# Retention and a gated feed-forward layer on one core: the order of three small products, and seven block products in place of eight for the second chunk

## The chip, the cores and the metric

The kernel runs on one core of a Trainium2 chip. A core has TensorE (matrix products, into PSUM), VectorE, ScalarE, GpSimd, and queues for the DMA engines. The metric is the device time of one execution in microseconds (us), smaller is better. In the listings of the profile PE is TensorE, PEld its loading of weights, DVE VectorE, ACT ScalarE, POOL GpSimd, SP the queue that issues most transfers.

## The reference

Eight batches, eight heads, 576 tokens, head size 64, all in float32. First comes a retention layer (attention with a decay in place of softmax), then a feed-forward layer with its own activation:

```python
# q, k, v: (8, 8, 576, 64); w_in: (512, 2048); w_out: (2048, 512)
scores = (1 / np.sqrt(64)) * np.matmul(q, k.transpose(0, 1, 3, 2))
gamma = 1.0 - 2.0 ** (-5.0 - np.arange(H))
Dmat = np.where(rel >= 0, gamma[:, None, None] ** rel[None], 0.0)   # rel = i - j
attn = np.matmul(scores * Dmat[None], v)
x = attn.transpose(0, 2, 1, 3).reshape(4608, 512)
h = x @ w_in
sp = np.maximum(h, 0.0) + np.log1p(np.exp(-np.abs(h)))             # softplus
g = h * erf(sp)
out = g @ w_out
```

The weights w_in and w_out arrive in double precision, and the kernel itself rounds them to float32 ("rounding" below).

## The kernel before

**Retention by pieces.** The 4608 tokens are cut into 36 pieces of 128. Within a piece the kernel computes masked scores; what earlier pieces of the same batch contribute comes through a state (64 by 64 for each head). Each piece i has three stages: `transposes(i)` brings q and k into the layout that the products need, `scores(i)` multiplies them and VectorE applies the mask, `outputs(i)` computes the piece's outputs and the new state:

```python
def outputs(i):
    ...
    o = [ps_at.tile([P, NP, P], FP32, tag="at", name=f"o{j}") for j in range(2)]
    for p in range(NP):                      # line 365: outputs within the piece
        for e in range(2):
            nc.tensor.matmul(o[p % 2][heads[(e + p) % 2], p // 2, :],
                lhsT=t["v"][:, 2 * p + e, :], rhs=t["sT"][:, e, p, :], ...)
    for state, r0, m in seen:                # line 376: what the state adds
        for p in range(NP):
            for e in range(2):
                nc.tensor.matmul(o[p % 2][heads[(e + p) % 2], p // 2, r0 : r0 + m],
                    lhsT=state[heads[e], p, :], rhs=t["qT"][heads[e], p, r0 : r0 + m], ...)
    if n == P:                               # line 388: the new state's product, k times v
        kv = flat(o[0])[:, 2 * P :].rearrange("p (a d) -> p a d", a=NP)
        for p in range(NP):
            for e in range(2):
                nc.tensor.matmul(kv[heads[e], p, :],
                    lhsT=t["k"][:, 2 * p + e, :], rhs=t["v"][:, 2 * p + e, :], ...)
    ...
    scaled(1)                                # VectorE: half of the outputs into x
    if n == P:
        sums = kv
        if s0 > 0:
            tt(sums, kv, kept[b], ALU.add)   # VectorE
        (nc.gpsimd if s0 > 0 else nc.vector).tensor_tensor(out=new, in0=sums, in1=gp, op=ALU.mult)
        kept[b] = new
    scaled(0)                                # VectorE: the other half
```

`seen` is empty in the first piece of a batch; the last piece of two batches at a time is shared by them (two states, no new state).

**The big products.** The tokens go through in nine chunks of 512, and the hidden columns in four groups (g = 0 to 3). For each group and chunk, `First` computes h, the activation is applied, and `Second` multiplies by w_out and adds to the output. Each is a product of 2 by 2 blocks. It is done by seven block products instead of eight, with sums of blocks made beforehand (Winograd's form of Strassen's method); VectorE makes the sums of x (`operands_x`), of the weights (`sums_in`, `sums_out`) and of g (`sums`). One block product is four `matmul` calls of 256 columns, which the profile records as eight. The first two chunks of the first group use the plain form instead, 16 steps of two calls:

```python
def plain(self):                             # line 550
    ...
    for dc in range(n_dc):
        slots = (A12, A22) if dc // 2 else (A11, S3)
        for n in range(4):
            for j in range(GP):
                nc.tensor.matmul(acc[n][:, ...], lhsT=wa[:, slots[n % 2], dc % 2, ...], rhs=t[:, dc, ...], ...)
            if dc == n_dc - 1:
                nc.scalar.copy(out=(self.t2 if tok else self.t1)[:, f], in_=acc[n])
            yield

def first(self):                             # the seven products, line 496
    self.product(A11, self.a, True);  nc.scalar.copy(out=self.t1[:, 0], in_=self.a)
    yield
    self.product(A12, e, True);       tt(self.t1[:, 0], e, self.t1[:, 0], ALU.add)
    yield
def middle(self):
    self.product(S2, self.a, False);  nc.scalar.copy(out=self.t1[:, 1], in_=self.a)
    yield
    self.product(S3, self.e, True)
    yield
    self.product(S1, self.a, False);  nc.scalar.copy(out=self.t2[:, 1], in_=self.a)
    tt(self.t2[:, 1], self.e, self.t2[:, 1], ALU.add)
    yield
def last(self):
    self.product(S4, self.a, False);  nc.scalar.copy(out=self.t2[:, 0], in_=self.a)
    yield
    self.product(A22, self.e, False); tt(self.t1[:, 1], self.e, self.t1[:, 1], ALU.add)
    self.softplus()
    yield

def operands_x(g, c):
    ...
    if g == 0 or c < PLAIN:                  # PLAIN = 2: chunks stored without the sums
        tt(t1, b12, b11, ALU.subtract)
        tt(t2, b22, t1, ALU.subtract)
        tt(b12, b22, b12, ALU.subtract)
    else:
        tt(t2, b12, b11, ALU.add)
        tt(t1, b22, t2, ALU.subtract)
    if g == 0:
        store_x(c)
    tt(t4, b21, t2, ALU.subtract)
```

**Rounding.** Each group has four parts of w_in and four of w_out. One part takes five steps: (1) two ScalarE instructions, (2) to (4) one VectorE instruction each, (5) a VectorE instruction and two on GpSimd (on VectorE for the first group's w_in). After the last part of w_out come four VectorE instructions for its sums; in the first group the four for w_in's sums come only behind those.

**The order of it all.** Engines work through their instructions in program order, so the program interleaves the work by hand. A string of letters steers the start (`a` one stage of attention, `p` one plain step of the first chunk, a digit so many rounding steps, `w` loading weights, `s` storing x). Then comes the second chunk:

```python
attend(after_chunk(1))                       # all stages that the second chunk needs
store_x(1)
for step, _ in enumerate(firsts[1].plain()):
    if step % 2 == 0:
        attend(min(done[0] + 1, most[0]))    # one stage of attention
    round_weights(int(step > 1))
    if step == 1:
        firsts[0].softplus(); firsts[0].erf()    # ScalarE, first chunk
    elif step == 5:
        firsts[0].multiply()                     # VectorE
    elif step == 8:
        firsts[0].sums()                         # VectorE
seconds[0].begin()
run(seconds[0].first(), (2, 2))              # a stage and two rounding steps with each product
firsts[1].softplus()
```

Of the kernel before, what the change touches and what calls it, by code (L numbers as in the profile page):

```python
# [2 lines left out]

# [1 line left out]

# [16 lines left out]
NP = H // 2  # L22
# [32 lines left out]
def kernel(  # L55
# [10 lines left out]
    nc = tc.nc  # L66
# [5 lines left out]
    n_dc = D_MODEL // P  # L72
    OH = D_MODEL // 2
    FH = D_FF // 2
    GP = 2
# [22 lines left out]
    def tt(out, in0, in1, op):  # L98
        nc.vector.tensor_tensor(out=out, in0=in0, in1=in1, op=op)  # L99

    def flat(ap):
        return ap.rearrange("p h d -> p (h d)")

    heads = [slice(e * D, (e + 1) * D) for e in range(2)]
# [87 lines left out]
    def parts():  # L192

        w2 = w_in.rearrange("(e c d) (h f) -> c e d h f", c=n_dc, d=D, h=2)
        for g in range(n_g):
            for dc in range(n_dc):
                a = A11 if dc < 2 else A12
                src = [(heads[(e + dc) % 2], w2[dc, e, :, :, 2 * g * GW : 2 * (g + 1) * GW]) for e in range(2)]

                yield src, "wa", g, a, dc % 2, ["wa"] if g > 0 and dc == n_dc - 1 else []  # L200
            for f in range(2):
                for j in range(GP):
                    ft = f * FH // P + g * GP + j
                    src = [(slice(0, P), w_out[ft * P : (ft + 1) * P, :].rearrange("p (h o) -> p h o", h=2))]
                    sums = (["wb"] if g > 0 else ["wb", "wa"]) if (f, j) == (1, GP - 1) else []
                    yield src, "wb", g, B21 if f else B11, j, sums

    def sums_in(a11, s3, a12, a22, s1, s2, s4):
# [79 lines left out]
    def round_weights(n=1):  # L288
        for _ in range(n):
            next(round_step, None)  # L290
# [9 lines left out]
    def x_tile():  # L300
        return xpool.tile([P, n_dc + 3, TCH], FP32, tag="x", name="x")
# [52 lines left out]
    def outputs(i):  # L354
        segments = pieces[i]
        t = live.pop(i)
        seen = [(kept[b], r0, n) for b, s0, n, r0 in segments if s0 > 0]

        b, s0, n, _ = segments[0]
# [3 lines that stand above are left out]
                nc.tensor.matmul(  # L365
                    o[p % 2][heads[(e + p) % 2], p // 2, :],
                    lhsT=t["v"][:, 2 * p + e, :],
                    rhs=t["sT"][:, e, p, :],
                    start=(p < 2),
                    stop=(not seen and p >= NP - 2),  # L370
                    skip_group_check=True,
                )
        for state, r0, m in seen:
            for p in range(NP):
                for e in range(2):
                    nc.tensor.matmul(  # L376
                        o[p % 2][heads[(e + p) % 2], p // 2, r0 : r0 + m],
                        lhsT=state[heads[e], p, :],
                        rhs=t["qT"][heads[e], p, r0 : r0 + m],
                        start=False,  # L380
                        stop=(p >= NP - 2),
                        skip_group_check=True,
                    )
        if n == P:
            kv = flat(o[0])[:, 2 * P :].rearrange("p (a d) -> p a d", a=NP)
            for p in range(NP):
                for e in range(2):
                    nc.tensor.matmul(  # L388
                        kv[heads[e], p, :],
                        lhsT=t["k"][:, 2 * p + e, :],  # L390
                        rhs=t["v"][:, 2 * p + e, :],
                        start=False,
                        stop=(p == NP - 1),
                        skip_group_check=True,
                    )
        c, at = i // PC, i % PC * P
        if (0, c) not in x:
            x[0, c] = x_tile()

        def scaled(j):  # L400
            to = x[0, c][:, j:NP:2, at : at + P]
            if c < n_ch - 1:
                by = (gq if n == P else gq2)[:, j::2, :].unsqueeze(2).to_broadcast([P, 2, P // n, n])
                dst, got = (y.rearrange("p a (m i) -> p a m i", i=n) for y in (to, o[j][:, :2]))
                tt(dst, got, by, ALU.mult)
                return

            for r0 in range(0, P, n):
                dst = to[:, :, r0 : r0 + n].rearrange("p h (r a) -> p h a r", r=SQ)
                got, by = (  # L410
                    y.rearrange("p h (a r) -> p h a r", r=SQ)
                    for y in (o[j][:, :2, r0 : r0 + n], (gq if n == P else gq2)[:, j::2, :])
                )
                tt(dst, got, by, ALU.mult)

        scaled(1)
        if n == P:
            sums = kv
            if s0 > 0:
                sums = att.tile([P, NP, D], FP32, tag="sums", name="sums")  # L420
                tt(sums, kv, kept[b], ALU.add)

            if b % 2 == 0 and s0 + P + D == S:
                new = att.tile([P, NP, D], FP32, tag="last", name="last", bufs=1)
            else:
                new = att.tile([P, NP, D], FP32, tag="state", name="state")
            (nc.gpsimd if s0 > 0 else nc.vector).tensor_tensor(out=new, in0=sums, in1=gp, op=ALU.mult)
            kept[b] = new
        scaled(0)
        load(i + 3, "kv")  # L430
        if i + 1 >= SQUARES:
            weigh_values(i + 1)
# [7 lines left out]
    done = [0]  # L440
# [5 lines left out]
    def after_chunk(c):  # L446

        return stages.index((outputs, (c + 1) * PC - 1)) + 1

    def attend(upto):  # L450
        while done[0] < min(upto, len(stages)):
            of, i = stages[done[0]]
            of(i)
            done[0] += 1

    PLAIN = 2

    def load_x(g, c):  # L460
        x[g, c] = x_tile()
# [2 lines left out]
    def store_x(c):  # L464
        nc.sync.dma_start(out=xd[c], in_=x[0, c][:, :n_dc])
# [3 lines left out]
    def operands_x(g, c):  # L469
        summed.add((g, c))  # L470
        t = x[g, c]
        b11, b12, b21, b22 = (t[:, 2 * d : 2 * d + 2, h * TH : (h + 1) * TH] for d in range(2) for h in range(2))
        t1, t2, t4 = (t[:, n_dc + j, :].rearrange("p (d i) -> p d i", d=2) for j in range(3))
        if g == 0 or c < PLAIN:
# [9 lines that stand above are left out]
        x[g, c] = {A11: b11, A12: b21, S4: b22, A22: t4, S1: t1, S2: t2, S3: b12}  # L484
# [240 lines left out]
    firsts = [First(g, c) for g, c in order]  # L725
    seconds = [Second(f) for f in firsts]
# [8 lines left out]
    def keep_busy(n):  # L735
        for _ in range(n):
            nc.tensor.matmul(idle[:, :P], lhsT=ones, rhs=ones, start=True, stop=True)
# [4 lines left out]
    def run(steps, rounds=(), stages=1):  # L742

        for step, _ in enumerate(steps):
            attend(min(done[0] + stages, most[0]))
            round_weights(rounds[step] if step < len(rounds) else 0)
# [4 lines left out]

    for what in "alkakakawkakakawwaa3awa2aaa5ppppaa5wwppa5ppawappwcppa5ppaaapp5s":
        if what == "a":
            attend(done[0] + 1)
        elif what == "p":
            next(products)
        elif what == "s":
            store_x(0)  # L760
        elif what == "l":
            load(2, "kv")
        elif what == "c":
            nc.sync.dma_start(out=cst[:, CONST_FIRST:], in_=consts[:, CONST_FIRST:])
        elif what == "w":
            load_weights()
        elif what == "k":
            keep_busy(2)
        else:
            round_weights(int(what))  # L770
    most[0] = before_chunk(3)
    attend(after_chunk(1))
    store_x(1)
    for step, _ in enumerate(firsts[1].plain()):
        if step % 2 == 0:
            attend(min(done[0] + 1, most[0]))
        round_weights(int(step > 1))
        if step == 1:
            firsts[0].softplus()
            firsts[0].erf()  # L780
        elif step == 5:
            firsts[0].multiply()
        elif step == 8:
            firsts[0].sums()
    seconds[0].begin()
    run(seconds[0].first(), (2, 2))
    firsts[1].softplus()
    most[0] = before_chunk(4)
    for b, nxt in zip(blocks[2:], blocks[3:] + [None]):
        n = order.index((b.g, b.c))  # L790
# [9 lines left out]
        elif n + 2 < n_s:  # L800
            f = firsts[n + 1]
# [62 lines left out]
```

## Time and profile before

| | before |
|---|---|
| median of three runs | 1027.61 us (1027.31 to 1028.06) |
| span of the profiled execution | 1024.0 us |
| TensorE matmul records, busy | 6348, 1017.6 us |
| VectorE instructions, busy | 1062, 667.6 us |
| ScalarE instructions, busy | 481, 390.2 us |
| GpSimd instructions, busy | 122, 122.6 us |

The busy time of an engine is the sum of what its instructions took. For TensorE, the end of a matmul is modelled, and a matmul that waits in the middle of a group makes the group look longer; the distance from one group's start to the next is the better measure. In a list in order of time, each line has the start, the time, the engine, the source line, the operation, what is written and read, the shape, and the number of instructions merged into it; a bracket at the end names an idle time before it and what ended it. In a list of waits, each line has who waited for whom, the total in us, how often, and the longest. A "wait for issue" is idle time for which the profile shows no partner.

### The profile page before, as it was taken

How to read it: one execution, taken by the hardware profiler on the slowest of the kernel's cores; microseconds unless marked ns; L12 is line 12 of the kernel's file. 1: busy time of each engine (PE TensorE's matmuls, PEld its weight loads, DVE VectorE, ACT ScalarE, POOL GpSimd, SP SyncE). 2: the span in 40 equal slices, each digit the busy share in tenths (PEclk: the TensorE clock that was granted, in tenths of full speed). 3: DMA queues.
4: the chain of work that ended last, by engine and by line, in shares of the span. 5: the costliest groups of instructions: out<-in, count | busy, mean ns of one | idle time of the engine just before them, and what ended most of it. 6: DMA issues, size and time to landing. Idle time of an engine off the chain costs nothing.

```text
span 1024.0 us, 15958 instructions
## 1 busy us (share of the span) xinstructions
PE 1017.6 (99%) x6348; PEld 876.0 (86%) x6348; DVE 667.6 (65%) x1062; ACT 390.2 (38%) x481; POOL 122.6 (12%) x122
## 2 busy tenths in 40 slices
PE   9999999999999999999999999999999999999998
PEld 8787888888888888888888888888888888888887
DVE  3769777976976656656666666666567655555555
ACT  3354134234134444334343444444433333333332
POOL 2143112122312110010001001000100000000000
PEclk9999999999999999999999999999999999999999
DMA  9998989979974354544444345444433333444434
GB/s 200 203 242 175 232 203 223 255 150 253 244 195 150 106 161 145 165 160 154 164 147 158 124 147 162 165 144 144 144 124 124 124 131 127 131 136 131 126 88 119
DMA packets 146986, 165.76 MB, mean 162 GB/s; under 512 B 97376, under 2 KB 121568, under 8 KB 138848
## 3 DMA queue, kind: packets, MB, share of 16 engines
q1 hardware_dynamic: 144832, 163.57, 56.4%
q10 hardware_dynamic: 2080, 1.18, 0.5%
q8 instruction: 50, 0.82, 0.4%
q14 instruction: 24, 0.20, 0.1%
HBM read 117.52 MB, written 47.19 MB: 161 GB/s over the span
## 4 chain that ended last, share of the span: by engine, by line
PE 94%; DMA 3%; DVE 2%; SPq 1%; POOL 1%; issue 0%; ACTq 0%; DVEq 0%; POOLq 0%
PE a L604 24%; PE a L496 23%; PE g L604 12%; PE g L496 12%; PE e L496 6%; PE e L604 6%; PE o L365 3%; PE s L347 3%; PE o L388 2%; DMA raw_k<-in_k_dram 1%; PE o L376 1%; DMA raw_v<-in_v_dram 1%; PE f L668 1%; SPq L147 1%; PE p L550 1%; PE h L668 1%
## 5 line engine op out<-in xcount | busy, mean ns | idle before, releaser
L496 PE MATMUL a<-x,wa 128*128 128x256 f32 x1088 | 258.3, 380 | 0.0
L496 PEld LDWEIGHTS a<-x,wa 128*128 128x128 f32 x1088 | 205.7, 190 | 28.5
L604 PE MATMUL a<-wb,s 128*128 128x256 f32 x840 | 200.0, 381 | 0.0
L604 PEld LDWEIGHTS a<-wb,s 128*128 128x128 f32 x840 | 158.4, 190 | 22.9 <-ACT o L618 0.7
L99 DVE TENSOR_TENSOR t<-g,t 128x512 f32<-128x512 f32 x68 | 47.0, 691 | 151.9 <-ACT t L526 114.1
L496 PE MATMUL g<-x,wa 128*128 128x256 f32 x544 | 129.2, 380 | 0.0
L496 PEld LDWEIGHTS g<-x,wa 128*128 128x128 f32 x544 | 102.8, 190 | 14.4
L99 DVE TENSOR_TENSOR o<-a,o 128x512 f32<-128x512 f32 x104 | 71.4, 687 | 46.4 <-PE a L604 46.4
L521 ACT COPY t<-a 128x512 f32<-128x512 f32 x34 | 19.9, 586 | 188.3 <-PE a L496 188.3
L99 DVE TENSOR_TENSOR t<-t,s 128x1024 f32<-128x1024 f32 x72 | 88.4, 1267 | 0.0
L274 POOL TENSOR_TENSOR wraw<-wraw 128x512 f32<-128x512 f32 x28 | 29.4, 1051 | 438.1 <-DVE wraw L272 184.4
L565 ACT ACTIVATE s<-t 128x1024 f32<-128x1024 f32 x72 | 72.1, 1049 | 24.6 <-DVE t L99 24.5
L99 DVE TENSOR_TENSOR x<-x 128x512 f32<-128x512 f32 x115 | 75.8, 693 | 1.2
L532 ACT COPY t<-a 128x512 f32<-128x512 f32 x34 | 19.9, 586 | 144.4 <-PE a L496 144.4
L569 ACT ACTIVATE s<-s 128x1024 f32<-128x1024 f32 x72 | 72.1, 1049 | 0.4
L604 PE MATMUL g<-wb,s 128*128 128x256 f32 x280 | 66.7, 381 | 0.0
L604 PE MATMUL e<-wb,t 128*128 128x256 f32 x280 | 66.6, 380 | 0.0
L604 PE MATMUL a<-wb,t 128*128 128x256 f32 x280 | 66.6, 380 | 0.0
L604 PE MATMUL g<-wb,t 128*128 128x256 f32 x280 | 66.4, 380 | 0.0
L99 DVE TENSOR_TENSOR sT<-s,cst 128x512 f32<-128x512 f32 x72 | 46.2, 682 | 30.4 <-PE s L347 30.4
L496 PE MATMUL e<-x,wa 128*128 128x256 f32 x272 | 64.8, 381 | 0.0
L99 DVE TENSOR_TENSOR o<-g,o 128x512 f32<-128x512 f32 x70 | 47.9, 684 | 20.9 <-ACT o L618 18.1
(86 smaller groups left out, 1247.1 us busy)
## 6 DMA issues: line engine op xcount, KB each, us to landing
od<-o SPq DMA_DIRECT2D x54, 512.0 KB, 3.3
x<-xd SPq DMA_DIRECT2D x27, 1024.0 KB, 4.8
o<-od SPq DMA_DIRECT2D x27, 1024.0 KB, 5.4
raw_qs<-in_q_dram SPq DMA_DIRECT2D x96, 112.0 KB, 4.4
raw_ks<-in_k_dram SPq DMA_DIRECT2D x84, 112.0 KB, 4.2
xd<-x SPq DMA_DIRECT2D x9, 1024.0 KB, 5.2
raw_v<-in_v_dram SPq DMA_DIRECT2D x64, 128.0 KB, 4.5
wraw<-in_moe_w_in_dram SPq DMA_DIRECT2D x32, 256.0 KB, 5.7
```

Source lines behind the costliest of these rows:

```text
L99: nc.vector.tensor_tensor(out=out, in0=in0, in1=in1, op=op)
L274: engine.tensor_tensor(out=r_f, in0=high_f, in1=r_f, op=ALU.mult)
L347: nc.tensor.matmul(ps[e][:, p, :], lhsT=t["kT"][heads[e], p, :], rhs=t["qT"][heads[e], p, :], start=True, stop=True)
L365: nc.tensor.matmul(o[p % 2][heads[(e + p) % 2], p // 2, :], lhsT=t["v"][:, 2 * p + e, :], rhs=t["sT"][:, e, p, :], start=(p < 2), stop=(no ...
L388: nc.tensor.matmul(kv[heads[e], p, :], lhsT=t["k"][:, 2 * p + e, :], rhs=t["v"][:, 2 * p + e, :], start=False, stop=(p == NP - 1), skip_gr ...
L496: nc.tensor.matmul(acc[:, j * TH : (j + 1) * TH], lhsT=weights["wa", self.g][:, a, d, j * P : (j + 1) * P], rhs=x[self.g, self.c][a][:, d, :],
L521: nc.scalar.copy(out=self.t1[:, 1], in_=self.a)
L532: nc.scalar.copy(out=self.t2[:, 0], in_=self.a)
L565: nc.scalar.activation(self.s[:, j], t, AF.Softplus)
L569: nc.scalar.activation(self.s[:, j], self.s[:, j], AF.Erf)
L604: nc.tensor.matmul(acc[:, tp, :], lhsT=left[:, j * TH + tp * P : j * TH + (tp + 1) * P], rhs=weights["wb", self.g][:, b, j, :], start=(sta ...
L668: nc.tensor.matmul(acc, lhsT=left[:, j * TH + tp * P : j * TH + (tp + 1) * P], rhs=weights["wb", self.g][:, b, j, :], start=(b in (B11, B2 ...
```

## The change

Two things are done. In `outputs`, the product for the new state moves directly behind the products for the outputs, and VectorE makes the sum for the new state ahead of both halves of the outputs; it is meant to give the next piece its state sooner. The second chunk now goes through the seven products like all later ones; for this the sums of w_in follow directly on its rounding, four more rounding steps stand in the steering string, one stage of attention is done ahead of the chunk, and the rounding steps are spread as 0, 2, 2, 2, 4, 2, 2 over the seven products, so that w_out is complete, with its sums, when `seconds[0]` begins. As x of the second chunk is now stored with its sums, the later groups make one sum fewer for it (`PLAIN = 1`).

```diff
-                yield src, "wa", g, a, dc % 2, ["wa"] if g > 0 and dc == n_dc - 1 else []
+                yield src, "wa", g, a, dc % 2, ["wa"] if dc == n_dc - 1 else []
...
-                    sums = (["wb"] if g > 0 else ["wb", "wa"]) if (f, j) == (1, GP - 1) else []
+                    sums = ["wb"] if (f, j) == (1, GP - 1) else []
...                                          (in outputs)
-        for state, r0, m in seen:
-            ...                              (line 376, moved)
         if n == P:
             kv = flat(o[0])[:, 2 * P :].rearrange("p (a d) -> p a d", a=NP)
             ...                              (line 388)
+        for state, r0, m in seen:
+            ...                              (line 376)
...
-        scaled(1)
         if n == P:
             sums = kv
             ...
             kept[b] = new
+        scaled(1)
         scaled(0)
...
-    PLAIN = 2
+    PLAIN = 1
...
-    for what in "alkakakawkakakawwaa3awa2aaa5ppppaa5wwppa5ppawappwcppa5ppaaapp5s":
+    for what in "alkakakawkakakawwaa3awa2aaa5ppppaa5wwppa5ppawappwcpp4a5ppaaapp5s":
...
     attend(after_chunk(1))
-    store_x(1)
-    for step, _ in enumerate(firsts[1].plain()):
-        if step % 2 == 0:
+    attend(done[0] + 1)
+    operands_x(0, 1)
+    f = firsts[1]
+    for step, _ in enumerate(chain(f.first(), f.middle(), f.last())):
+        if step > 0:
             attend(min(done[0] + 1, most[0]))
-        round_weights(int(step > 1))
-        if step == 1:
+        round_weights((0, 2, 2, 2, 4, 2, 2)[step])
+        if step == 0:
             firsts[0].softplus()
             firsts[0].erf()
-        elif step == 5:
+        elif step == 2:
             firsts[0].multiply()
-        elif step == 8:
+        elif step == 4:
             firsts[0].sums()
     seconds[0].begin()
-    run(seconds[0].first(), (2, 2))
-    firsts[1].softplus()
+    run(seconds[0].first())
```

More of the change, by code (lines that the diff above doesn't have):

```diff
@@ L2 @@
 from contextlib import ExitStack
+from itertools import chain
 import numpy as np
@@ L372, in outputs @@
                 )
-        for state, r0, m in seen:
[L374 to L383, printed above, removed]
         if n == P:
@@ L393, in outputs @@
                         stop=(p == NP - 1),
+                        skip_group_check=True,
+                    )
+        for state, r0, m in seen:
+            for p in range(NP):
+                for e in range(2):
+                    nc.tensor.matmul(
+                        o[p % 2][heads[(e + p) % 2], p // 2, r0 : r0 + m],
+                        lhsT=state[heads[e], p, :],
+                        rhs=t["qT"][heads[e], p, r0 : r0 + m],
+                        start=False,
+                        stop=(p >= NP - 2),
                         skip_group_check=True,
```

## The prediction

> **What bounds the kernel now.** I read the page first, then TensorE's waits, then its list of instructions in order of time, and last the lists of VectorE and ScalarE beside it. From the page, the busy shares and the chain that ended last:
>
> ```profile
> PE 1017.6 (99%) x6348; PEld 876.0 (86%) x6348; DVE 667.6 (65%) x1062; ACT 390.2 (38%) x481; POOL 122.6 (12%) x122
> ...
> PE 94%; DMA 3%; DVE 2%; SPq 1%; POOL 1%; issue 0%; ACTq 0%; DVEq 0%; POOLq 0%
> ```
>
> TensorE never stops for long, and the chain is TensorE. But a busy TensorE is not one at its peak: a matmul that waits inside a group shows as a longer group. So I used the distance between starts. TensorE in order of time (start, modelled length, line; line 347 is the scores, 365 the outputs, 376 the product with the state, 388 the new state's product, 496 and 604 the big products):
>
> ```profile
> 84.59 0.60 PE L332 MATMUL pt_k<-ident,raw_k 128*128 128x128 f32 x4
> 85.03 1.89 PE L604 MATMUL e<-wb,t 128*128 128x256 f32 x8
> 86.85 1.61 PE L365 MATMUL o<-sT,raw_v 128*64 128x128 f32 x16
> 88.39 0.67 PE L376 MATMUL o<-qT,state 64*64 64x128 f32 x16
> ...
> 114.08 1.09 PE L365 MATMUL o<-sT,raw_v 128*64 128x128 f32 x16
> 115.00 0.63 PE L388 MATMUL o<-raw_v,raw_k 128*64 128x64 f32 x16
> 115.56 1.99 PE L496 MATMUL a<-x,wa 128*128 128x256 f32 x8
> ...
> 165.41 1.09 PE L365 MATMUL o<-sT,raw_v 128*64 128x128 f32 x16
> 166.44 0.67 PE L376 MATMUL o<-qT,state 64*64 64x128 f32 x16
> 167.03 0.69 PE L388 MATMUL o<-raw_v,raw_k 128*64 128x64 f32 x16
> 167.65 1.99 PE L496 MATMUL g<-x,wa 128*128 128x256 f32 x8
> ```
>
> The outputs at 86.85 took 1.54 us to the next start (88.39) where undisturbed ones take 1.03: a stall of 0.51, and VectorE's mask just then ran from 86.04 to about 87.3. The rest is even. From 98.5 to 311.9 us, where attention lies between products, every kind of step repeats to 0.01 us; after 314 us a product of eight records follows the other at 1.73 us with two exceptions of 0.10, until the last at 1018.49. So nothing off TensorE matters after 98 us, and the end moves by what TensorE's work and its stalls before 98 us change, plus a small amount for each later piece of attention.
>
> **The skill.** Trainium skill, "TensorE: Matmul & The Clock Gate", section The mechanism: a weight load overlaps running matmuls of another row group, each tile of the array holding its own weights. The trace shows gaps where the tile shape changes; TensorE's weight loads waited:
>
> ```profile
> PEld o L365 <- issue: 10.4, 33, 0.5
> PEld s L347 <- issue: 9.0, 27, 0.3
> PEld o L376 <- issue: 4.8, 28, 0.2
> PEld o L388 <- issue: 3.6, 21, 0.2
> ```
>
> The fourth line is what I need. Line 388 runs in 32 pieces; 24 follow line 376, eight follow line 365 at once, and the 21 waits are about as many as the first kind. Both 365 and 388 are 128*64, 376 is 64*64. Second, "SBUF — State Buffer", section Who interferes with whom: a VectorE instruction with two SBUF inputs blocks against a GpSimd one that reads SBUF. The trace agrees: one such 128x512 instruction at 76.00 took 1.77 us and not 0.69, with GpSimd's add at 75.81 lasting 1.41. Third, "ScalarE: Activation LUTs", section What ACT_TABLE_LOAD costs: about 1283 ns; the trace has 1.28.
>
> **Part 1: seven products for the second chunk.** Before: 16 steps of four records, 64 records. After: seven products of eight, 56. Eight records by 1.73/8 = 0.216 us take **1.73 us** off TensorE, all of it on the path. One stage of attention now stands next to another and not between products; each entry or exit of such a run costs a product 0.10 (1.73 alone, 1.83 with one, 1.92 with both), so I take another 0.15.
>
> **Part 2: order inside the outputs.** Before, a piece with a state costs 1.03 (365 to 376) + 0.60 (376 to 388) + 0.615 (388 to a product) = 2.24 us. After, 365 to 388 is 0.92, as at 114.08. Then 388 to 376: 388 alone is 0.565, as at 115.00, plus the 0.10 that 365 pays when 376 follows = 0.665. Then 376 to a product: I take 0.55 to 0.60, since it now is 0.60 toward 388, and half-width ones part from a product with 0.34 against 0.28 between themselves. Sum 2.14 to 2.19, a gain of 0.05 to 0.10 each; VectorE's instruction "sums" has count 24, so 24 such pieces: 1.2 to 2.4, middle **1.8 us**. The stated purpose, an earlier state, brings nothing: no line of TensorE's waits names the state.
>
> **Part 3: VectorE and ScalarE from 60 to 98 us.** In that stretch VectorE is busy 31.05 of 38.00 us. Added: four combinations of x (4 x 0.69 = 2.8, start to start nearer 2.4) and three additions from PSUM (3 x 0.69 = 2.1). Removed: the sums of w_in, which filled 89.07 to 90.4 and 91.95 to 94.3, about 3.8 us with blocking; they move to the gap of 3.45 us ahead of 49.54 and cost nothing there. VectorE so carries some 32 us in a stretch that TensorE wants to make 2 us shorter. The trouble is its order:
>
> ```profile
> 64.22 1.29 DVE L99 TENSOR_TENSOR sT<-s,cst 128x512 f32<-128x512 f32 x2 [1.69 <-PE s L347]
> 69.21 0.43 DVE L259 TENSOR_SCALAR wb<-wb 128x512 f32<-128x512 f32 x1 [3.69 <-ACT wb L254]
> ...
> 79.02 0.68 DVE L99 TENSOR_TENSOR s<-t,s 128x512 f32<-128x512 f32 x1
> 79.62 0.42 DVE L263 TENSOR_SCALAR wb<-wb 128x512 uint32<-128x512 uint32 x1
> 79.96 0.70 DVE L326 STREAM_TRANSPOSE qT<-raw_qs 128x512 f32<-128x512 f32 x1
> ```
>
> The rounding at 69.21 waits until ScalarE has done softplus and erf with two table loads (1.28 + 2.00 + 1.28 + 2.00, from 61.98 to 68.5). That stays about the same, since ScalarE still starts near 62. From there I laid the new order end to end with these lengths: rounding and transpose to 71.7; multiplication 2.3 to 74.0; outputs, rounding, addition and mask to 76.8; four rounding steps 1.85 to 78.7; four sums of the first chunk 2.4 plus 1.1 blocked by GpSimd to 82.2; transpose of tenth q to **82.9**. TensorE reaches the scores of that piece, now behind the first product of the second stage, at about **81.4**: stall 1.5 us. Before that, the fifth product needs the accumulator that ScalarE copies behind the rounding's two instructions (69.0 to 70.2, copy to 70.8), while TensorE is there at 70.35: stall 0.6. Other small ones 0.3. Set against these, the present stalls of 0.27 (scores at 80.81) and 0.51 (outputs at 86.85) go or are counted in: net **+1.6 us**, the most uncertain term.
>
> **Sum.** -1.73 - 0.15 - 1.8 + 1.6 = -2.1 us; 1027.6 - 2.1 = 1025.5.
>
> **Later.** One VectorE addition fewer for the second chunk in each of three later groups (three instead of four) is off the path: no stalls there.
>
> **Rivals.** (a) VectorE becomes the bound of the stretch: a lag of 4 us at the tenth transpose eats both gains, and the time is 1027.5 to 1028.5. For it: VectorE's 31 of 38 us, its strict order, waits for GpSimd. Against: about 3.7 of the idle time stands in one place ahead of 69.21, and x's combinations fit in there; the removed sums of w_in free 3.8 us at 89 to 94, where a lag is made good. (b) The stalls don't come and both gains stay: 1023.5 to 1024. For it: before, VectorE was equally full from 70 to 80 us (4.96 and 4.97 of 5.00) and TensorE stalled 0.27. Against: the tenth transpose now has four rounding steps, two additions and the combinations ahead of it. (c) The order inside the outputs brings nothing, as the two shape changes only move (376 to a product costs what 388 to a product did plus one change): 1027.3. Against: the eight direct cases of line 388 have no weight-load wait.
>
> **Range and chances.** The order is -1.2 to -2.4, the products -1.7 to -1.9, the stalls 0 to +4. The centre is 1025.5, the low end is all gains with few stalls (1023.2), the high end heavy stalls that eat everything (1027.9). Two per cent would be 20 us; nothing here is near, since only about 38 us of the run can be disturbed at all: faster 0.01, within 0.98, slower 0.01.
>
> **What would show it.** Right: 6340 matmul records; after 100 us each piece of attention with a state takes 2.14 to 2.19 us from 365 to the following product, and 388 follows 365 after 0.92; the weight-load waits before 388 are gone; the first product of the third chunk starts 1 to 1.5 us sooner than 98.51; a stall of about 1.5 us at the tenth scores, waiting for the transposed q. Wrong: pieces at 2.24 (part 2 fails), no stall at the tenth scores (then lower), or a third chunk at 99 us or later (then higher), or new stalls after 100 us, which I exclude.

## The result, and the profile after

| | before | changed |
|---|---|---|
| median | 1027.46 us (1026.00 to 1028.31) | 1029.92 us (1029.09 to 1032.58) |
| ratio to before | 1 | 1.003 (95% interval 1.0016 to 1.0044) |
| span of the profiled execution | 1024.0 us | 1030.8 us |
| TensorE matmul records | 6348 | 6340 |

The change costs 0.3%. The profiled execution of the changed kernel was its longest; I use it for mechanisms and the medians for sizes. In its lines the new state's product is line 377 and the product with the state line 388. Two counts are in use: the piece called the tenth, here and in the recorded texts, is i = 10 in the program, while the eighth and the 13th piece are i = 7 and i = 12. TensorE in order of time, where the change was to gain and where it lost:

```profile
81.02 1.99 PE L604 MATMUL a<-wb,t 128*128 128x256 f32 x8
86.65 2.08 PE L347 MATMUL s<-qT,kT 64*128 64x128 f32 x16 [3.63 <-DVE qT L326]
88.66 3.78 PE L604 MATMUL e<-wb,t 128*128 128x256 f32 x8
92.23 0.96 PE L332 MATMUL pt_k<-ident,raw_k 128*128 128x128 f32 x4
93.03 1.89 PE L604 MATMUL a<-wb,s 128*128 128x256 f32 x8
...
101.88 1.09 PE L365 MATMUL o<-sT,raw_v 128*64 128x128 f32 x16
102.80 0.63 PE L377 MATMUL o<-raw_v,raw_k 128*64 128x64 f32 x16
103.36 0.67 PE L388 MATMUL o<-qT,state 64*64 64x128 f32 x16
103.96 1.99 PE L496 MATMUL a<-x,wa 128*128 128x256 f32 x8
```

The last four lines are the gain: 0.92 + 0.56 + 0.60 = 2.08 us from the outputs to the next product, against 2.24. TensorE's weight loads, which waited 21 times ahead of the new state's product, 3.6 us in all, have no such wait left in the list. The lines above are the loss. The tenth scores wait 3.63 us for the transposed q. Then, with no wait named, the scores take 2.01 us to the next start and not 1.09, the product 3.57 and not 1.83, the transposes 0.80 and not 0.44: 3.0 us more. The busy time by stretches shows the clock (PE, PEld, DVE, ACT and POOL with their counts, then TensorE's granted clock, the DMA share and GB/s):

```profile
80.00:85.00 5.00, 3.02 (x36) 2.39 (x32) 4.93 (x6) 0.00 (x0) 4.07 (x3) 1.00 0.04 6
85.00:90.00 5.00, 3.35 (x19) 2.98 (x20) 4.90 (x10) 1.49 (x2) 0.34 (x1) 0.61 0.41 114
90.00:95.00 5.00, 5.00 (x20) 3.87 (x21) 3.18 (x6) 1.62 (x4) 0.00 (x0) 0.70 0.87 181
```

The clock fell behind the wait: in slices of 1 us it is 0.50 from 87 to 92 us and 1.00 again from 93 us. The Trainium skill ("TensorE: Matmul & The Clock Gate", Part 1) says that the clock is halved after an idle window of some 3.4 us; I had read nothing of it into the prediction. VectorE, third of the engines, is full from 80 to 90 us (4.93 and 4.90 of 5.00). What filled it (VectorE in order of time, the combinations of x, then the four sums of the activation ahead of the tenth transpose):

```profile
63.53 5.41 DVE L100 TENSOR_TENSOR x<-x 128x512 f32<-128x512 f32 x4
...
80.62 0.68 DVE L100 TENSOR_TENSOR s<-t 128x512 f32<-128x512 f32 x1
81.34 1.41 DVE L100 TENSOR_TENSOR s<-s,t 128x512 f32<-128x512 f32 x1
82.67 1.76 DVE L100 TENSOR_TENSOR s<-t,t 128x512 f32<-128x512 f32 x1
84.36 1.52 DVE L100 TENSOR_TENSOR s<-t,s 128x512 f32<-128x512 f32 x1
85.81 0.70 DVE L326 STREAM_TRANSPOSE qT<-raw_qs 128x512 f32<-128x512 f32 x1
```

The same four sums took 3.6 us in the kernel before (76.00 to 79.62 us), and 5.2 us here. And a second loss, far behind the place of the change, in what I had called even:

```profile
238.12 1.16 PE L347 MATMUL s<-qT,kT 64*128 64x128 f32 x16 [1.82 <-DVE kT L326]
239.21 3.31 PE L496 MATMUL g<-x,wa 128*128 128x256 f32 x8
242.32 2.30 PE L496 MATMUL a<-x,wa 128*128 128x256 f32 x8
```

TensorE waits 1.82 us for a transposed k, and again a slow clock follows: 3.11 and 2.23 us for products that take 1.83, with a granted clock of 0.50 from 240 to 243 us. VectorE in turn waited for the load of that k:

```profile
236.88 1.10 DVE L326 STREAM_TRANSPOSE kT<-raw_ks 128x512 f32<-128x512 f32 x1 [1.93 <-DMA raw_ks<-in_k_dram]
```

### The profile page after: what moved, and what is told of

Read it like the earlier page. It is cut to its first block, busy times and chain, and to the rows that moved or that the text cites. A ratio compares the mean times of both kernels' runs of the same rounds, so it can differ in the third digit from the quotient of the medians.

```text
span 1030.8 us, 15943 instructions
## 1 busy us (share of the span) xinstructions
PE 1016.5 (99%) x6340; PEld 878.0 (85%) x6340; DVE 673.2 (65%) x1066; ACT 390.1 (38%) x481; POOL 123.2 (12%) x122
## 4 chain that ended last, share of the span: by engine, by line
PE 86%; DMA 7%; DVE 3%; SPq 3%; issue 1%; POOL 0%; ACT 0%; DVEq 0%; POOLq 0%
PE a L604 22%; PE a L496 22%; PE g L604 11%; PE g L496 11%; PE e L604 6%; PE e L496 5%; DMA raw_v<-in_v_dram 3%; PE s L347 2%; PE o L365 2%; DMA wraw<-in_moe_w_in_dram 1%; SPq L148 1%; DMA raw_qs<-in_q_dram 1%; PE o L388 1%; SPq L132 1%; DMA raw_ks<-in_k_dram 1%; PE o L377 1%
## 5 line engine op out<-in xcount | busy, mean ns | idle before, releaser
L496 PE MATMUL a<-x,wa 128*128 128x256 f32 x1120 | 266.5, 381 | 0.3 <-DVE x L100 0.3
L496 PEld LDWEIGHTS a<-x,wa 128*128 128x128 f32 x1120 | 211.9, 190 | 30.5 <-issue 0.7
L496 PE MATMUL g<-x,wa 128*128 128x256 f32 x560 | 134.3, 383 | 0.0
L496 PEld LDWEIGHTS g<-x,wa 128*128 128x128 f32 x560 | 106.4, 191 | 15.1 <-issue 0.2
L100 DVE TENSOR_TENSOR x<-x 128x512 f32<-128x512 f32 x116 | 79.3, 717 | 1.2
L604 PEld LDWEIGHTS e<-wb,t 128*128 128x128 f32 x280 | 53.9, 194 | 8.1 <-issue 0.4
## 6 DMA issues: line engine op xcount, KB each, us to landing
x<-xd SPq DMA_DIRECT2D x27, 1024.0 KB, 4.8
o<-od SPq DMA_DIRECT2D x27, 1024.0 KB, 4.9
xd<-x SPq DMA_DIRECT2D x9, 1024.0 KB, 5.0
```

Source lines behind the costliest of these rows:

```text
L496: nc.tensor.matmul(acc[:, j * TH : (j + 1) * TH], lhsT=weights["wa", self.g][:, a, d, j * P : (j + 1) * P], rhs=x[self.g, self.c][a][:, d, :],
L604: nc.tensor.matmul(acc[:, tp, :], lhsT=left[:, j * TH + tp * P : j * TH + (tp + 1) * P], rhs=weights["wb", self.g][:, b, j, :], start=(sta ...
```

## The experiments

All medians are beside 1027.1 to 1027.7 us of the kernel before on the same chip. The edits are shown in part.

**Each part alone.** Theory A: the order gains, VectorE's lag and the slow clock lose. Theory B: VectorE's new order in the first pieces eats the gain. The order alone (on the kernel before):

```diff
+        # line 388 ahead of line 376; VectorE: sums and new state, then scaled(1), scaled(0)
```

> The kernel before with only the order inside the outputs changed: the new state's product behind the outputs, and VectorE's sum ahead of both halves. Theory A (the order is a gain, the loss of the whole change is VectorE's lag in the second chunk and a lower TensorE clock behind it): the changed kernel's trace shows 0.92 + 0.56 + 0.60 = 2.08 us for a piece with a state against 2.24, 24 such pieces, so 3.7 us less: 1023.5 to 1024.5. Theory B (VectorE's new order delays the first pieces, where TensorE waited 0.74 us at 24 us and 0.41 us at 42 us): the gain is eaten, 1026.5 to 1028.

Measured: 1026.71, ratio 0.9992 (0.9985 to 0.9998). A gain, but 0.65 us and not 3.7. The time is theory B's, and its reason holds for a part. With the new order TensorE meets a wait ahead of these outputs:

```profile
42.83 1.53 PE L365 MATMUL o<-sT,raw_v 128*64 128x128 f32 x15 [0.41 <-issue]
```

From the start of the plain product ahead of them (`pg`) to the transposes behind them, TensorE takes 4.06 or 4.07 us in all eleven runs with the new order, and 3.88 to 3.94 in the four with the old one: a loss of 0.12 to 0.19 us where 0.15 should be won. The larger part of what is missing is the loads', as the runs without v show below.

The other part alone (the changed kernel with the old order):

```diff
-        # line 388 ahead of line 376
+        # line 376 ahead of line 388; VectorE: scaled(1), sums and new state, scaled(0)
```

> The changed kernel with the old order inside the outputs (on TensorE and VectorE): only the second chunk by seven products and the rounding sooner. Theory A: the stall of about 3.6 us at the tenth scores and the slow clock for about 5.6 us behind it stay, so that it is slower than the changed kernel by the 3.7 us of the order: 1032 to 1034, and slower than the kernel before by 5 or 6 us. Theory B: about as the kernel before less 1.7 us of products, 1025.5 to 1027.

Measured: 1032.18, ratio 1.0049 (1.0037 to 1.0061). So the seven products for the second chunk lose 4.8 us by themselves. The wait at the tenth scores is there (4.1 us), and is not the order's doing. Beside this part the order is worth 2.3 us (1032.18 to 1029.92), more than alone.

**The sums out of the transpose's way.**

```diff
-        elif step == 4:
+        elif step == 6:
             firsts[0].sums()
```

> The changed kernel with VectorE's four sums of the first chunk's activation moved from behind the fifth product to behind the seventh, so that the transpose of the tenth q stands ahead of them on VectorE. Theory A: the transpose ends near 81.5 us instead of 86.5, TensorE comes to the tenth scores at 83 and waits for nothing, a wait of up to 1.5 us may come up at the product with the second sum; the clock stays at 1.00 if no wait is over 3 us: 6.6 us less than the changed kernel less up to 1.5, so 1023 to 1025. Theory B: the sums' place matters little, 1029 to 1030.

Measured: 1029.49, ratio 1.0019. The tenth scores wait for nothing, and the transpose stands at 80.43 us; the wait has moved to the product that needs the second sum, and is longer than I expected:

```profile
89.20 2.45 PE L604 MATMUL a<-wb,s 128*128 128x256 f32 x8 [2.28 <-DVE s L100]
91.58 1.98 PE L365 MATMUL o<-sT,raw_v 128*64 128x128 f32 x16
93.34 0.92 PE L377 MATMUL o<-raw_v,raw_k 128*64 128x64 f32 x16
```

A wait of 2.28 us brought the slow clock too (outputs 1.76 us and not 0.92). So the order of VectorE's work says where TensorE waits. That it waits at all comes, it seems, from the amount; no run takes work away from VectorE there.

**The wait filled.**

```diff
         ps = [ps_at.tile(...) for e in range(2)]
+        if i == 10:
+            for _ in range(14):
+                nc.tensor.matmul(ps[0][:, 0, :], lhsT=ones, rhs=ones, start=True, stop=True)
```

> The changed kernel, with 14 idle products (128 columns, about 0.22 us each, some 3.1 us) on TensorE ahead of the tenth scores, written to a bank that the scores overwrite. They fill the wait for the transposed q and do nothing else. Theory A, with the lower clock caused by the idle time: the stall stays as long, but no slice behind it shows a clock under 1.00, and the time falls by the 3.0 us that scores, product and transpose took longer (0.92 + 1.74 + 0.36): 1026 to 1027.5. Rival: the lower clock has another cause (it comes at this load anyway): no change, 1029 to 1030.5.

Measured: 1030.58, ratio 1.003 (1.0018 to 1.0042), no less than the changed kernel. The mechanism is as expected: the clock is 1.00 throughout, and scores and product behind the filled wait have their usual lengths (1.10 and 1.83 us between starts):

```profile
81.68 3.29 PE L347 MATMUL s<-ones 128*128 128x128 f32 x28
85.98 1.16 PE L350 MATMUL s<-qT,kT 64*128 64x128 f32 x16 [1.02 <-DVE qT L326]
87.08 1.99 PE L607 MATMUL e<-wb,t 128*128 128x256 f32 x8
88.91 0.60 PE L332 MATMUL pt_k<-ident,raw_k 128*128 128x128 f32 x4
```

The third chunk starts at 101.41 us and not at 103.96. But by the medians nothing of this reached the end (between the two profiled executions, of which the changed kernel's is its longest, 2.0 us did): between 200 and 280 us TensorE waited five times, 3.7 us in all, three of them for a transposed k. Theory A lacked something.

**GpSimd in VectorE's way.**

```diff
-            engine = nc.vector if (name, g) == ("wa", 0) else nc.gpsimd
+            engine = nc.vector if g == 0 else nc.gpsimd
```

> The changed kernel, with the two last instructions of rounding for the first group's w_out on VectorE in place of GpSimd (as w_in's already are). It adds two 128x512 instructions (some 0.7 us each) for each of four parts to VectorE and takes GpSimd away while VectorE combines x and sums the activation. Theory G (in the changed kernel GpSimd's instructions block VectorE's with two SBUF inputs: the four combinations of x took 5.41 us and the four sums 5.2, against 2.4 to 2.8 alone): both fall to 2.5 to 3.8, the tenth transpose comes 1 to 2 us sooner, the wait ahead of the tenth scores falls from 3.6 to about 2, the time to about 1028. Rival: they are slow for another reason (their own length, SBUF): they stay over 5 us, VectorE gets later by the 2.8 us added ahead of the tenth scores, the wait grows to 6 us, 1032.

Measured: 1031.82, ratio 1.0041. VectorE in order of time:

```profile
65.40 2.91 DVE L100 TENSOR_TENSOR x<-x 128x512 f32<-128x512 f32 x4
...
83.42 0.68 DVE L100 TENSOR_TENSOR s<-t 128x512 f32<-128x512 f32 x1
84.14 0.69 DVE L100 TENSOR_TENSOR s<-s,t 128x512 f32<-128x512 f32 x1
84.75 0.68 DVE L100 TENSOR_TENSOR s<-t,t 128x512 f32<-128x512 f32 x1
85.35 0.68 DVE L100 TENSOR_TENSOR s<-t,s 128x512 f32<-128x512 f32 x1
85.95 0.70 DVE L326 STREAM_TRANSPOSE qT<-raw_qs 128x512 f32<-128x512 f32 x1
```

Combinations 2.91 us and not 5.41, sums 2.5 us and not 5.2: half of their length was GpSimd's. Theory G is right on the lengths and wrong on the time: the two instructions added for each part cost VectorE as much, and the tenth transpose ends no sooner (86.65 and 86.51 us). TensorE came later too and waited 2.47 us for it.

**More rounding ahead of the chunk, sums split.**

```diff
-    "...wcpp4a5ppaaapp5s"
+    "...wcpp4a5ppaaa5pp5s"
-        round_weights((0, 2, 2, 2, 4, 2, 2)[step])
+        round_weights((0, 0, 0, 1, 4, 2, 2)[step])
-        elif step == 4:
-            firsts[0].sums()
+        elif step == 5:
+            firsts[0].sums((0,))             # sums((1,)) behind the second stage's first product
```

> The changed kernel, with the third part of w_out rounded ahead of the second chunk (five steps moved there from the chunk, into idle time of VectorE of some 3.5 us between 52 and 60 us), and with the sums of the first chunk's activation split: the two that are needed first behind the tenth transpose, the other two behind the first product of the second stage. Theory A (the loss lies in VectorE's order from 60 to 94 us, and in the slow clock behind the wait): no wait over 1.5 us at the tenth scores and behind it, clock 1.00, the third chunk starts at 97 to 99 us: 1025 to 1027. Rival B (VectorE is full there whatever its order): the wait moves to the next product, as it did when all four sums were moved, 1028 to 1030.

Measured: 1028.95, ratio 1.0018 (1.001 to 1.0027). In between. The clock stays at 1.00 in the profiled execution and no wait is over 1.3 us, but there are three (0.82, 1.28, 1.17), and the third chunk starts at 100.81. The third part's rounding did not go into idle time: it stood right ahead of the combinations, which took 5.42 us again. The median is rival B's.

**The loads.** Theory Q: SyncE's queue, which in the run of the order alone issues transfers for 195 of 214 us between 98 and 312 us, can't issue sooner. Theory D: the work of the DMA engines sets the pace. The row loads go to ScalarE's queue, in the first run with the new order, in the second with the old one:

```diff
-                queue = nc.scalar if (name, i) == ("k", 0) else nc.sync
+                queue = nc.scalar if (name, i) == ("k", 0) or i >= SQUARES_K else nc.sync
```

> The order inside the outputs alone, and from the 13th piece on the row loads of k and v (four transfers a piece) are issued by ScalarE's queue and not by SyncE's, which from 98 to 312 us issues for about 195 of 214 us. Theory Q (the 0.154 us a piece won on TensorE is lost again because SyncE's queue can't issue the loads sooner; TensorE waits for transposed k at about 233 and 272 us): those waits go, and the order's gain shows: 1023.5 to 1025. Rival D (the 16 DMA engines, busy to about 0.92 in that stretch, set the pace): the loads land no sooner, 1026 to 1027. Rival S: the transfers that ScalarE issues delay its copies out of PSUM: 1027 or more.

> The kernel before with only the same row loads on ScalarE's queue. Theory Q: there is little wait for loads to remove as TensorE is slower by just that, so 1026 to 1027.4, and the order's gain is the difference between this one and the one with both, 2 us or more. Rival D: as the kernel before, 1027.4, and no difference larger than that of the order alone (0.7 us).

Measured: 1054.7 (ratio 1.0271) and 1056.08 (1.0292). Theories Q and D missed, and of rival S only the open bound holds: TensorE waits 19.1 and 19.0 us for transposed k, not for ScalarE's copies. The waits of SyncE's queue in the first of the two:

```profile
SPq L131 <- DMA raw_k<-in_k_dram: 57.1, 25, 8.1
```

SyncE's queue now waits, 25 times, for the landing of rows that ScalarE's queue issued. I only note that; whether issuing was the limit this pair can't tell.

So I took load away. In the next runs the rows of v are not loaded from the 13th piece on, and GpSimd weighs a column of ones in their place:

```diff
+                elif name == "v" and i >= SQUARES_K:
+                    t["v"] = ones[:, :1].unsqueeze(2).to_broadcast([P, H, D])
```

> The order inside the outputs alone, and the rows of v are not loaded from the 13th piece on (GpSimd weighs a column of ones in their place, so those pieces' outputs are not attention outputs): it leaves out two of the twelve transfers that SyncE's queue issues for such a piece, everything else stays. Theory L (loads set the pace of the pieces between 98 and 312 us, and ate the order's gain there): TensorE's waits for transposed k at 233 and 272 us go, and the time is 1023 to 1024.5, some 2 to 3 us under the order alone. Rival: the loads are not what holds it, 1026 to 1027.

> The kernel before with the same v rows left out, as the control. Theory L: its TensorE waits little for loads, so little is gained: 1026 to 1027.4; the order's gain with the loads lightened is the difference to the run above, 16 pieces by 0.154 = 2.5 us after 98 us, up to 3.7 in all. Rival: both fall alike, the difference stays at the 0.7 us of the order with all loads.

Measured: 1024.23 (ratio 0.9967, 0.9954 to 0.998) with the new order, 1027.06 (0.9995, 0.9987 to 1.0003) with the old one. The order is worth 2.83 us where these loads don't interfere, 0.65 where they do, as theory L has it. The order with all loads, and without the rows of v:

```profile
99.51 1.99 PE L496 MATMUL a<-x,wa 128*128 128x256 f32 x8
232.94 1.16 PE L347 MATMUL s<-qT,kT 64*128 64x128 f32 x16 [1.09 <-DVE kT L326]
98.00:312.00 214.00, 212.05 (x2056) 175.30 (x2053) 168.12 (x282) 64.53 (x86) 48.02 (x49) 1.00 0.93 219
...
99.08 1.99 PE L501 MATMUL a<-x,wa 128*128 128x256 f32 x8
98.00:312.00 214.00, 214.00 (x2099) 176.81 (x2096) 168.70 (x283) 64.53 (x85) 49.91 (x51) 1.00 0.78 193
```

TensorE, first of the engines, is busy for 212.05 of the 214.00 us with all loads, and for all of them without the rows of v.

> The changed kernel with the v rows not loaded from the 13th piece on (as in the two runs of that kind; those pieces' outputs are not attention outputs). Theory L: the loads no longer pace the stretch from 98 to 312 us, TensorE's 1.8 us wait for transposed k near 238 us goes, the stall at the tenth scores and the slow clock behind it stay: 1026.5 to 1028, some 2 to 3 us over the order alone without those loads (1024.2). Rival: 1029 to 1030, as with the loads.

> The same, and with the 14 idle products ahead of the tenth scores. With the loads out of the way, what the filled wait is worth must show: theory A (waiting idle lowers TensorE's clock for some 5 us, which costs about 2 us in a typical execution) expects 1.5 to 3 us less than the run above and a clock of 1.00. Rival (the slow clock costs nothing that counts): the same time as above.

Measured: 1028.16 and 1026.87. The changed kernel without those loads is 3.93 us over the order alone (1024.23), all of it the second chunk's part. Filling the wait brings 1.29 us of this back, less than the 1.5 to 3 expected. In the profiled executions scores, product and transposes behind the wait are 2.7 us shorter with it, but a new wait of 0.86 us for ScalarE's copy comes at the next product (90.64 us). From the third chunk's first product to the last outputs, the stretch is 213.43 us with the old order (99.58 to 313.01), and 211.02 in all three with the new one (99.08 to 310.10, 103.17 to 314.19, 101.67 to 312.69). The difference, 2.41 us, is 16 pieces by 0.151. With all loads the same stretch is 213.43 us for the kernel before, 213.17 for the order alone, 214.60 for the changed kernel and 215.50 for the changed kernel with the old order. Ahead of the stretch lie the other eight pieces with a state: 1.23 us by 0.154, and 0.50 measured (99.58 to 99.08).

> The order alone, v rows from the 13th piece on not used, but their transfers still issued, as many as before with 8 rows and 4 columns each instead of 128 (or 64) rows and 64 columns. Theory Q (it is the number of transfers that SyncE's queue issues one after the other): as the order with all loads, 1026 to 1027. Theory D (their size, the work of the DMA engines or of writing descriptors): as without them, 1024 to 1024.7.

```diff
+                    few = raw.tile([P, H, 4], FP32, tag="few", name="raw_few", bufs=8)
+                    # the same number of transfers, 8 rows and 4 columns each, not used
```

Measured: 1024.3 (0.9951 to 0.9976), the stretch again 211.02. The number of transfers alone is not it. But smaller transfers change three things at once. From 98 to 312 us the DMA share is 0.93 with the order alone, and 0.78 without the v rows (0.76 with the tiny ones). SyncE's queue also issues for 169 us with the tiny ones and not for 195. And no one reads the tiny tiles, so their transfers wait for no buffer of v. Which of the three holds the loads is not shown; theory Q, if it means the queue's time, stays open.

## Why the prediction was wrong, step by step

By the medians the change splits into four steps: without the v rows the kernel before goes from 1027.46 to 1027.06 us, the order takes it to 1024.23, the second chunk's part to 1028.16, and with the v rows back it is 1029.92. The prediction had -1.8 for the order and -0.3 for the second chunk's part (products, one run of attention fewer, waits). Both signs that it named for a higher time came: the third chunk after 99 us (103.96), and a new wait after 100 us (238.12).

- **Part 1, products.** Right: eight records fewer.
- **Part 2, order.** Right in kind, too small in size: 0.154 us a piece, not 0.05 to 0.10. I had put 0.10 on line 388's step to line 376, as lines 365 and 376 have it between them; it is 0.564, no more than to a product. But 24 x 0.154 = 3.7 us is what TensorE's steps get shorter; 2.83 arrived without the v rows and 0.65 with them. "So nothing off TensorE matters after 98 us" failed here: a faster TensorE ran into its loads, which had just been in time. In the changed kernel this costs 1.8 us (1028.16 to 1029.92).
- **Part 3, waits.** This is the step that turned a gain into a loss: a net of +1.6 us was expected. Between the outputs of the eighth piece and the third chunk (58.55 to 103.96, 45.41 us against 41.03) the account is: products -1.73, one run of attention fewer -0.15, order -0.46 (three pieces), waits of 0.34 and 0.53 for x and the mask, **3.63** at the tenth scores, **3.02** by the slow clock, less the old 0.78: +4.4, and 4.38 were measured. So waits and clock, less the old waits, are +6.7 in this execution. The wait was 3.63 and not 1.5 because the tenth transpose ended at 86.5 us and not at 82.9, while TensorE was there 1.6 us later than laid out (83.0 us). VectorE was 1.2 us behind the plan when the rounding went on (70.87 us), lost 0.8 in four rounding steps (2.7 for 1.85) and 1.7 in the sums (5.2 for 3.5). I had found the blocking by GpSimd, had it in one of eight instructions, and left the combinations at 2.4 us. They took 5.41 and kept VectorE busy until just before the rounding; but ScalarE, whose softplus began at 63.66 us and not near 62, gave the rounding its operand only at 70.84, and with short combinations (2.91 us) VectorE waited there 1.10 us for ScalarE. The 0.6 us at the fifth product (0.45 by the prediction's own times) didn't come.
- **The slow clock** was in no term. It is 1.3 us by the filled wait (1028.16 to 1026.87), at least, as filling brought a new wait; in the profiled execution it is 3.0.
- **Rivals.** (a), VectorE as the bound with a lag of 4 us at the tenth transpose, was right (3.6 us), and even its 1028.5 was too low. From 60 to 90 us VectorE is busy 29.45 of 30 us; before it had 5.4 us idle in two gaps there. I let those gaps speak against it; they were smaller than what was put in (5.41 for the combinations and 2.1 for three additions). (b) is out by the wait of 3.63 us, (c) by the 2.83 us of the order.
- **The state.** An earlier state shows no gain: no wait of TensorE names it, before or after.

Open: the first outputs of the eighth piece start 1.07 us later than before in the profiled execution in spite of five shorter pieces, with a 0.91 us wait for a load of q at 33.97 us (0.29 before). The new order's own loss near 42 us is a part of it. Two profiled executions of kernels with the old order and none of the second chunk's part differ by as much at the third chunk (98.51 and 99.58 us), so I put no cause to the rest. Open too is why the part alone, with the old order, also waits for k (0.92 and 0.88 us near 239 and 278 us) where the kernel before did not.

The best of these with nothing left out is the order alone: 1026.71 us, under both kernels.

## What to carry to other kernels

Before giving a full engine more work in a stretch, sum its work there with the durations it has under contention, not its shortest ones; reordering then only moves the wait. A wait of a few microseconds on TensorE costs more than its length if the clock falls behind it. And where a trace shows no wait for loads, ask how much earlier they could have come: a gain on the busiest engine may be lost there at once.

## What the hardware showed

- Putting the two small products of one tile shape next to each other saved time on TensorE: with 128*64, 128*64, 64*64 in place of 128*64, 64*64, 128*64 a piece took 2.08 and not 2.24 us. The 128*64 group of 128 columns took 0.92 us to the next start ahead of its own shape and 1.03 ahead of 64*64; the 128*64 group of 64 columns took 0.56 ahead of 64*64 and ahead of a 128*128 product alike. That the shapes are the cause is argued from these distances.
- Four fp32 additions or subtractions of 128x512 took VectorE 5.41 us (combinations) and 5.2 us (sums) with GpSimd at work beside them, and 2.91 and 2.5 us in the run that took the rounding from it.
- The clock fell behind waits of 1.82, 2.28, 2.47 and 3.63 us, and not behind waits of 1.02, 1.09 and 1.16 us. The length of the wait alone does not decide it: with the rows on ScalarE's queue the clock fell behind a wait of 1.74 us (25.69 us), and with rounding on VectorE it did not behind one of 1.80 us (237.73 us). The skill's page has about 3.4 us of idle time for it; here less was enough.
- How long the clock stayed low did not follow the wait. Its shortfall from 1.00, added up over slices of 1 us, is 1.70 or 1.71 us behind waits of 1.74, 1.82, 2.28, 2.47, 3.43 and 3.52 us (behind the second, 0.14 + 3 x 0.50 + 0.07), which is 3.4 us at 0.50. Behind waits of 3.63 and 4.11 us it is 3.41 or 3.42 us, which is 6.8 us at 0.50.
